# Float64 weights made float32 in two VectorE passes instead of three, with the words between them in a PSUM bank, and the low word's three bits by arithmetic on GpSimd

## The chip, the cores and the metric

The kernel runs on 1 core of one Trainium2 chip. The metric is the device time of one execution in microseconds, the median of several runs. A core has five engines with a queue of instructions each: TensorE (PE in the profile; PEld is its weight load), VectorE (DVE), ScalarE (ACT), GpSimd (POOL) and SyncE (SP), which here issues the DMAs. SBUF is the working memory; PSUM has eight banks of 512 float32 words per partition, into which TensorE writes.

## The reference

Windowed attention with 8 heads over 8 sequences of 576 positions, and then a feed-forward step with three up-projections of which the largest value is taken. The four weight matrices arrive as float64.

```python
scores = scale * np.matmul(q, k.transpose(0, 1, 3, 2))        # (8, 8, 576, 576), head_dim 64
# heads 0-3 see the last 32 keys, heads 4-7 every fourth of the last 128
scores = np.where(masks[None, :, :, :], scores, -1000000000.0)
attn = np.exp(scores - np.max(scores, axis=-1, keepdims=True))
attn = attn / (np.sum(attn, axis=-1, keepdims=True) + 1e-09)
x = np.matmul(attn, v)                                          # to (4608, 512)
h = np.maximum(np.maximum(x @ w1, x @ w2), x @ w3)              # w1, w2, w3: (512, 768)
out = h @ w_out                                                 # (768, 512)
```

## The kernel before

**Three kinds of work.** *Weights*: 24 chunks of the up-projections, 128 x 384 float64 numbers each, and 12 chunks of the down-projection, 128 x 256 each (`weight`, line 355). A chunk comes by DMA into a staging buffer `st`, is turned into float32, and is kept as two float32r parts, a high one (`wupH`, `wdn[:, 0]`) and a low one (`wupL`, `wdn[:, 1]`). *Attention*: 64 units of one half sequence (288 queries) and two heads (`attention`, line 432). The first 12 units are "lean": their scores come from plain float32 products. A later unit splits queries and keys into two parts `F` first. A unit's steps are scores into a bank `s` (TensorE), mask and row minimum (VectorE), exponential with row sum (ScalarE), reciprocal (VectorE), normalisation (GpSimd, or VectorE), transposition of the probabilities (TensorE for the first 8 units, into `pt`; then VectorE, line 672, into one of three buffers `PT`), products with the values into a bank `pv` (TensorE, line 684), and a copy `xH` (ScalarE or VectorE) and a remainder `xL` (VectorE) into a ring of four halves. *FFN*: 12 tiles of 384 tokens (`ffn`, line 715). A tile has 216 products `u` (line 729; 6 groups `f`, each needs 4 up chunks), whose maxima `tmp` VectorE takes, whose float32r parts `h` ScalarE and GpSimd make, and then 54 products `d` with the down weights (line 784) in three blocks of 128 tokens.

**How float64 becomes float32.** A float64 number is two 32-bit words, the low one first. Four steps work on the words: `rebias` (line 386; ScalarE, VectorE or GpSimd) reads the high word as if it were a float32 and multiplies it by 2^-112; `shift` (line 396, VectorE) drops the sign and moves the result up by three bits; `low` (line 399, VectorE) puts the low word's upper three bits under it; `sign` (line 407, VectorE) puts the sign back. All four write the same SBUF tile `c` (one of five buffers). Then `split` and a subtraction (line 423, GpSimd or VectorE) make the two float32r parts.

**What sets the order.** Nothing is written out by hand: `Plan.order` (line 147) gives each engine, by a rough clock with a cost per step, the step that is due first among those whose inputs and buffers are there. Steps that several engines can do carry a cost for each. The FFN's products are chained one after the other, and the due times of the other steps follow from theirs. So a change of a step's cost, engine or buffers moves the steps of all engines. Each engine then runs its queue in that order, with waits where the data or a buffer needs them.

**Banks.** `BANKS` (line 302) gives the eight PSUM banks to tags: scores `s` 2, `pt` 1, `pv` 2, FFN 3. A `pv` bank is free again when `xH` and `xL` of its unit have been read from it.

Of the kernel before, what the change touches and what calls it, by code (L numbers as in the profile page):

```python
# [10 lines left out]
U32 = mybir.dt.uint32  # L11
I64 = mybir.dt.int64
AF = mybir.ActivationFunctionType
ALU = mybir.AluOpType
# [13 lines left out]
# the first units have their scores from plain float32 products: fewer elementwise steps  # L28
# while the tensor engine has time
LEAN = 12  # L30
LEAN_B = -(-LEAN // (2 * NPAIR))
# up to this unit the tensor engine transposes the probabilities, then the vector engine
TURN = 8
# up to this half each head of a unit has its reciprocals apart
APART = 4
# buffers of the padded queries, and the unit up to which every other one's keys take a buffer of "F"
QPADS, KEYS_F = 4, 8
# weights are staged in the buffers of the down weights, every STAGE_H-th of those before STAGE_F in one of "h"
STAGE_F, STAGE_H = 13, 3
# the order of issue, in the plan's microseconds  # L40
SPILL = 2  # how much later its usual engine must be before a step goes to another
TO_PE = 0.26  # slack for inputs of the tensor engine
FFN_PACE = 1.267  # time that the FFN's products are given, over their own
UNIT_PACE, UNIT_SLACK, UNIT_LEAD = 1.146, 3.85, 3.484  # the same of attention, its margin, and a unit's to the next
# [3 lines left out]
def blocks_of(hf, dil):  # L48
    """Query blocks of one head's half: (first query column, queries, first key column, keys, mask offset)."""
# [22 lines left out]
class Buf:  # L72
    """A tile that a pool hands out when the first step that uses it is issued."""
# [16 lines left out]
class Step:  # L90
    """Instructions that one engine runs in a row; costs holds the engines that can, the usual one first."""
# [11 lines left out]
class Plan:  # L103
    """Puts the steps of all engines in an order of issue: each engine takes, of the steps whose
    inputs and buffers are there by a rough clock, the one that is due first. The waits that the
    data needs are Tile's."""
# [17 lines left out]
    def deadlines(self):  # L124
        """When steps are due: the FFN's products one after the other, the others as these need them."""
# [21 lines left out]
    def order(self):  # L147
# [11 lines left out]
        while len(order) < len(self.steps):  # L159
# [33 lines left out]
            else:  # L193
                cost = st.costs[e]
                if e == "pe":
                    # the tensor engine's clock is halved after a tick of its monitor that saw little work
# [39 lines left out]
def tile_dilated_window_attention__then__maxout_ffn(  # L236
# [41 lines left out]
    # key column kk is seen by query row qq when qq < kk <= qq + WIN  # L278
# [23 lines left out]
    BANKS = {"s": 2, "pt": 1, "pv": 2, "ffn": 3}  # L302
# [14 lines left out]
    # outside its band PT stays zero for good  # L317
# [31 lines left out]
    # ---------------------------------------------------------------- weights  # L349
# [5 lines left out]
    def weight(j, before):  # L355
        """Columns of float64 weights, turned into float32 and split into two float32r parts."""
# [15 lines left out]
        cb = buf("tmp", f"c{j}")  # L372
# [4 lines left out]
        def cf():  # L377
            return cb.t[:, :n]
# [3 lines left out]

        def like(ap):
            return ap.rearrange("p (g m) -> p g m", g=3) if up else ap

        def rebias(e):
            # the exponent's difference of 1023 - 127 is 112 units of the high word's own, which is 1/8 as fine
            h = st.t.rearrange("p (n t) -> p n t", t=2)[:, :, 1]
            if e == "act":
                nc.scalar.mul(cf(), h, REBIAS)  # L390
            elif e == "pool":
                nc.gpsimd.tensor_scalar(cf(), h, REBIAS, 1.0, ALU.mult, ALU.mult)
            else:
                nc.vector.tensor_scalar(cf(), h, REBIAS, None, ALU.mult)

        def shift(_):
            nc.vector.tensor_scalar(cw(), cw(), 0x0FFFFFFF, 3, ALU.bitwise_and, ALU.logical_shift_left)  # L397
# [497 lines left out]
```

## Time and profile before

| what | value |
|---|---|
| runs before | 775.7, 773.89, 774.74 us; median 774.74 |
| span of the profiled execution | 775.4 us |
| TensorE busy in the span | 730.6 us, 94% |
| VectorE, ScalarE, GpSimd busy | 482.5, 384.0, 406.4 us |
| mean granted TensorE clock | 0.978 |
| bytes moved | 72.75 MB, mean 94 GB/s |

The span goes from the first to the last instruction of one execution that was profiled on the chip. No separate time is listed for that execution; its span of 775.4 us lies between the slowest run and the median, 0.7 us above the median. Busy time is the time in which an engine works on an instruction, a wait inside an instruction included; a group's "mean ns" is the mean length of one instruction, and instructions that follow each other on one engine overlap a little in these records.

### The profile page before, as it was taken

What the parts mean: (1) busy time and instruction counts of PE and PEld (TensorE: products, weight loads), DVE (VectorE), ACT (ScalarE), POOL (GpSimd) and SP (SyncE); (2) the same over time, 40 slices, a digit from 0 to 9 for tenths busy, and PEclk for the clock granted to TensorE, in tenths of its full rate; (3) what the DMA queues carried; (4) which work ended last, traced back from release to release, by engine and by line L of the source; (5) the groups of instructions that cost most, each with busy time, mean ns of one, the idle gap of its engine ahead of it and who ended that gap; (6) DMA issues with size and microseconds to landing.
All of it is one profiled execution on the core that took longest, in us unless ns stands there. A gap on an engine that the chain in (4) does not pass through costs nothing.

```text
span 775.4 us, 14660 instructions
## 1 busy us (share of the span) xinstructions
PE 730.6 (94%) x4724; PEld 670.2 (86%) x4724; DVE 482.5 (62%) x1865; ACT 384.0 (50%) x1324; POOL 406.4 (52%) x560
## 2 busy tenths in 40 slices
PE   6787589999999999999999999999999999999998
PEld 5676578998998899799799799899699799899996
DVE  6899998888988879643884887511895611011110
ACT  7666466776766667552566477511465211111111
POOL 5877676787788588671288288611176011011110
PEclk9779898999999999999999999999999999999999
DMA  6974144344444433330433342410330200100001
GB/s 192 283 240 145 47 128 135 99 132 135 122 126 134 131 103 107 120 94 23 127 92 96 121 138 66 129 31 1 95 115 33 71 14 0 41 1 14 28 1 41
DMA packets 41516, 72.75 MB, mean 94 GB/s; under 512 B 4320, under 2 KB 15584, under 8 KB 41440
## 3 DMA queue, kind: packets, MB, share of 16 engines
q1 hardware_dynamic: 41440, 71.81, 30.3%
q8 instruction: 38, 0.62, 0.3%
q14 instruction: 38, 0.31, 0.1%
HBM read 62.36 MB, written 9.44 MB: 93 GB/s over the span
## 4 chain that ended last, share of the span: by engine, by line
PE 74%; DVE 19%; issue 3%; DMA 2%; POOL 1%; ACT 1%; SPq 0%; ACTq 0%; POOLq 0%; DVEq 0%
PE u L729 49%; PE d L784 15%; DVE PT L672 5%; PE s L533 5%; PE pv L684 3%; DVE c L408 3%; DVE c L400 3%; DVE W L560 2%; PE s L524 2%; DVE F L332 1%; DVE tmp L332 1%; DVE c L397 1%; DVE xL L332 1%; DMA st<-in_w_up_dram 1%; DVE W L546 1%
## 5 line engine op out<-in xcount | busy, mean ns | idle before, releaser
L332 POOL TENSOR_TENSOR F<-raw,F 64x288 fp32r<-64x288 f32 (+3 forms) x192 | 166.1, 867 | 81.2 <-ACT F L325 38.6
L332 DVE TENSOR_TENSOR tmp<-u,tmp 128x384 f32<-128x384 f32 x144 | 79.9, 555 | 203.0 <-PE u L729 200.4
L566 ACT ACTIVATE W<-W,mx 96x128 f32<-96x128 f32 (+3 forms) x448 | 166.5, 373 | 79.0 <-DVE mx L560 78.3
L729 PE MATMUL u<-xH,wupH 128*128 128x384 f32 x864 | 188.5, 339 | 7.2 <-DVE tmp L332 4.9
L729 PE MATMUL u<-xL,wupH 128*128 128x384 f32 x864 | 187.3, 338 | 0.0
L729 PE MATMUL u<-xH,wupL 128*128 128x384 f32 x864 | 186.4, 337 | 0.0
L332 POOL TENSOR_TENSOR h<-tmp,h 128x384 fp32r<-128x384 f32 x72 | 73.7, 1023 | 202.7 <-ACT h L325 201.7
L784 PE MATMUL d<-wdn,h 128*128 128x512 f32 x648 | 163.8, 401 | 0.0
L729 PEld LDWEIGHTS u<-xH,wupH 128*128 128x128 f32 x864 | 152.0, 189 | 11.2 <-DVE tmp L332 6.7
L729 PEld LDWEIGHTS u<-xL,wupH 128*128 128x128 f32 x864 | 152.1, 189 | 0.4
L729 PEld LDWEIGHTS u<-xH,wupL 128*128 128x128 f32 x864 | 151.5, 189 | 0.3
L672 DVE STREAM_TRANSPOSE PT<-W 32x192 f32<-32x192 f32 (+1 forms) x336 | 134.8, 401 | 13.0 <-PE pv L684 7.5
L784 PEld LDWEIGHTS d<-wdn,h 128*128 128x128 f32 x648 | 119.5, 191 | 24.6
L332 POOL TENSOR_TENSOR W<-W,sm 96x384 f32<-96x384 f32 (+2 forms) x127 | 103.5, 830 | 25.0 <-DVE sm L626 22.8
L325 ACT CAST h<-tmp 128x384 fp32r<-128x384 f32 x72 | 36.8, 511 | 131.2 <-DVE tmp L332 131.1
L566 ACT ACTIVATION_READ_ACCUMULATOR W<-W,mx 72x1 f32 (+1 forms) x448 | 84.1, 188 | 0.0
L325 ACT CAST F<-raw 128x576 fp32r<-128x576 f32 (+2 forms) x103 | 72.1, 704 | 18.2 <-DMA raw<-in_qk_d_dram 8.7
L560 DVE CUSTOM_DVE_ANT_0 W<-W,s 96x128 f32<-96x128 f32 (+2 forms) x364 | 76.6, 252 | 1.2
L546 DVE TENSOR_TENSOR W<-s,mask 72x208 f32<-72x208 f32 (+2 forms) x158 | 53.8, 361 | 28.2 <-PE s L533 26.1
L533 PE MATMUL s<-F 128*96 128x256 f32 (+3 forms) x364 | 59.9, 266 | 7.4 <-DVE mx L560 6.5
L533 PEld LDWEIGHTS s<-F 128*72 128x72 f32 (+1 forms) x364 | 47.0, 151 | 20.2 <-DVE mx L560 5.5
L684 PEld LDWEIGHTS pv<-PT,v 104*64 104x64 f32 (+1 forms) x896 | 36.6, 142 | 27.6 <-issue 15.3
(47 smaller groups left out, 502.6 us busy)
## 6 DMA issues: line engine op xcount, KB each, us to landing
raw<-in_qk_d_dram SPq DMA_DIRECT2D x28, 352.0 KB
st<-in_w_up_dram SPq DMA_DIRECT2D x24, 384.0 KB
out_dram<-o SPq DMA_DIRECT2D x36, 256.0 KB
raw<-in_qk_p_dram SPq DMA_DIRECT2D x28, 304.0 KB
raw<-in_qk_p_dram SPq DMA_DIRECT2D x24, 288.0 KB
raw<-in_qk_d_dram SPq DMA_DIRECT2D x24, 288.0 KB
v<-in_v_d_dram SPq DMA_DIRECT2D x32, 208.0 KB
v<-in_v_p_dram SPq DMA_DIRECT2D x32, 192.0 KB
```

Of the source, the lines that this page charges most:

```text
L325: nc.scalar.copy(dst, src)
L332: (nc.vector if eng == "dve" else nc.gpsimd).tensor_tensor(dst, a, b, op=op)
L400: nc.vector.scalar_tensor_tensor(cw(), words()[:, :, 0], 29, cw(), op0=ALU.logical_shift_right, op1=ALU.bitwise_or)
L408: nc.vector.scalar_tensor_tensor(cw(), words()[:, :, 1], 0x80000000, cw(), op0=ALU.bitwise_and, op1=ALU.bitwise_or)
L533: nc.tensor.matmul(bank.t[:nq, 256 * z : 256 * z + 2 * nk], f[:, q0 : q0 + nq], kv[:, :, k0 : k0 + nk], start=True, stop=True,)
L546: nc.vector.tensor_tensor(W3()[:nq, n0 : n0 + 2, mo : mo + nk], s3[:, :, :nk], m, op=ALU.add)
L560: nc.vector.tensor_tensor_reduce(a, x, y, -0.125, 3e38, ALU.add, ALU.min, mx.t[:nq, n : n + 1])
L566: nc.scalar.activation(a, a, AF.Exp, bias=mx.t[:nq, n : n + 1], scale=-1.0, accum_out=sm.t[:nq, n : n + 1])
L672: nc.vector.transpose(PT.t[c : c + 32, : 2 * nb, 32 * i : 32 * i + 32], W3(e)[32 * i : 32 * i + 32, :, c - e : c - e + 32],)
L684: nc.tensor.matmul(pv.t[64 * j : 64 * j + 64, q0 : q0 + nq], v.t[:wk, j, i, :], PT.t[:wk, nb * j + i, :nq], start=True, stop=True,)
L729: nc.tensor.matmul(bank.t[:, :n], wt[:, 3 * f + g, c, :], (xL if xz else xH)[:, c, r0 : r0 + n], start=(m == 0 and c == 0), stop=(m == 2 a ...
L784: nc.tensor.matmul(bank.t, hs[f].t[:, hz, s0 : s0 + 128], wdn[f].t[:, wz], start=(f == 0 and m == 0), stop=(f == NF - 1 and m == 2),)
```

## The change

`shift` and `low` go. `rebias` writes a tile `cp` in PSUM instead of `c`, and can run on ScalarE or VectorE only. A new step `low3` works on the staging buffer alone: it reads the byte that holds the low word's upper three bits, multiplies it by 1/32 and subtracts 31/64, and writes the result as an integer over the low word. GpSimd is its usual engine, VectorE the other. `joined` (VectorE) shifts the word in PSUM up by three bits, which drops the top bits, and puts the three bits under it, in place in PSUM. `sign` (VectorE) reads PSUM and the staging buffer and writes `c` in SBUF. `cp` has one bank, and `pv` has one where it had two. The costs that the plan is given are those that the steps of the same kind had. Comments were taken out as well, which moves line numbers by 1 to 12.

```diff
-    BANKS = {"s": 2, "pt": 1, "pv": 2, "ffn": 3}
+    BANKS = {"s": 2, "pt": 1, "pv": 1, "c": 1, "ffn": 3}
...
-        cb = buf("tmp", f"c{j}")
+        cb, cp = buf("tmp", f"c{j}"), buf("c", f"cp{j}")
...
             if e == "act":
-                nc.scalar.mul(cf(), h, REBIAS)
-            elif e == "pool":
-                nc.gpsimd.tensor_scalar(cf(), h, REBIAS, 1.0, ALU.mult, ALU.mult)
+                nc.scalar.mul(pf(), h, REBIAS)
             else:
-                nc.vector.tensor_scalar(cf(), h, REBIAS, None, ALU.mult)
-
-        def shift(_):
-            nc.vector.tensor_scalar(cw(), cw(), 0x0FFFFFFF, 3, ALU.bitwise_and, ALU.logical_shift_left)
-
-        def low(_):
+                nc.vector.tensor_scalar(pf(), h, REBIAS, None, ALU.mult)
+
+        def low3(e):
+            b = st.t.bitcast(U8).rearrange("p (n t) -> p n t", t=8)[:, :, 3]
+            (nc.gpsimd if e == "pool" else nc.vector).tensor_scalar(
+                words()[:, :, 0], b, 1 / 32, -31 / 64, ALU.mult, ALU.add
+            )
+
+        def joined(_):
             nc.vector.scalar_tensor_tensor(
-                cw(), words()[:, :, 0], 29, cw(), op0=ALU.logical_shift_right, op1=ALU.bitwise_or
+                pw(), pw(), 3, words()[:, :, 0], op0=ALU.logical_shift_left, op1=ALU.bitwise_or
             )
...
             nc.vector.scalar_tensor_tensor(
-                cw(), words()[:, :, 1], 0x80000000, cw(), op0=ALU.bitwise_and, op1=ALU.bitwise_or
+                cw(), words()[:, :, 1], 0x80000000, pw(), op0=ALU.bitwise_and, op1=ALU.bitwise_or
             )
...
-        first = s = plan.add({"act": act(n), "dve": dve(n), "pool": pool1(n)}, rebias, [s, before], [st, cb])
-        s = plan.add({"dve": dve2(n)}, shift, [s], [cb])
-        s = plan.add({"dve": dve(n)}, low, [s], [st, cb])
-        s = plan.add({"dve": dve(n)}, sign, [s], [st, cb])
+        first = plan.add({"act": act(n), "dve": dve(n)}, rebias, [s, before], [st, cp])
+        s = plan.add({"pool": pool1(n), "dve": dve(n)}, low3, [s, before], [st])
+        s = plan.add({"dve": dve(n)}, joined, [s, first], [st, cp])
+        s = plan.add({"dve": dve(n)}, sign, [s], [st, cp, cb])
```

The plan puts all 36 `low3` on GpSimd, 31 `rebias` on ScalarE and 5 on VectorE. The order moves on every engine. Three places:

**VectorE, around the first `tmp` of the first tile.** Before, a row with `tmp` as its output takes a maximum of the first tile, and nearly all else are weight passes:

```order
L400 SCALAR_TENSOR_TENSOR c_761<-st_293,c_761 128x384
L397 TENSOR_SCALAR c_776<-c_776 128x384
L408 SCALAR_TENSOR_TENSOR c_761<-st_293,c_761 128x384
L400 SCALAR_TENSOR_TENSOR c_776<-st_693,c_776 128x384
L397 TENSOR_SCALAR c_789<-c_789 128x384
L408 SCALAR_TENSOR_TENSOR c_776<-st_693,c_776 128x384
L332 TENSOR_TENSOR tmp_0_811<-u_0_1_793,tmp_0_811 128x384
```

Now, at the same first `tmp`:

```order
L412 SCALAR_TENSOR_TENSOR cp_843<-cp_843,st_658 128x384
L638 RECIPROCAL sm_729<-sm_729 96x3 x2
L420 SCALAR_TENSOR_TENSOR c_867<-st_658,cp_843 128x384
L638 RECIPROCAL sm_821<-sm_821 72x4
L330 CAST F_1_879<-raw_1_779 128x608
L333 TENSOR_TENSOR F_0_804<-raw_0_718,F_0_804 64x288
L333 TENSOR_TENSOR F_1_879<-raw_1_779,F_1_879 128x320
L333 TENSOR_TENSOR tmp_0_857<-u_0_1_846,tmp_0_857 128x384
```

The weight passes of a chunk now stand one after the other, and attention of later units (`F`, and below it masks and transposes) stands between the chunks.

**GpSimd, in the second half of the up chunks.** Before, the low parts of the weights (`wupL`) and little else:

```order
L332 TENSOR_TENSOR wupL<-c_837,wupH 128x3x128
L332 TENSOR_TENSOR wupL<-c_858,wupH 128x3x128
L332 TENSOR_TENSOR W_87<-W_87,sm_703 96x384
L332 TENSOR_TENSOR wupL<-c_882,wupH 128x3x128
L332 TENSOR_TENSOR W_87<-W_87,sm_703 96x384
L332 TENSOR_TENSOR h_1_963<-tmp_1_901,h_1_963 128x384
```

Now:

```order
L333 TENSOR_TENSOR wupL<-c_1092,wupH 128x3x128
L406 TENSOR_SCALAR st_881<-st_881 128x384
L333 TENSOR_TENSOR F_1_1134<-raw_1_1011,F_1_1134 128x320
L406 TENSOR_SCALAR st_973<-st_973 128x384
L333 TENSOR_TENSOR wupL<-c_1136,wupH 128x3x128
L333 TENSOR_TENSOR h_2_1167<-tmp_2_1080,h_2_1167 128x384
L633 TENSOR_TENSOR sm_1003<-sm_1003,eps_c 96x3
L333 TENSOR_TENSOR F_0_1027<-raw_0_901,F_0_1027 64x288
```

A `low3` (output `st`) per chunk came in, and the `F` remainders of later units.

**TensorE, at the end of the first tile's down products.** Rows `d_128` and `d_256` are the second and third block. Before:

```order
L784 MATMUL d_128_1428<-wdn_1366,h_5_1359 128x512 x3
L684 MATMUL pv_1501<-PT_93,v_1388 64x72 x8
L784 MATMUL d_256_1517<-wdn_1125,h_0_870 128x512 x3
L533 MATMUL s_2_1528<-F_1_1414 96x256 x2
L784 MATMUL d_256_1517<-wdn_1169,h_1_963 128x512 x3
```

Now:

```order
L796 MATMUL d_0_1525<-wdn_1735,h_5_1550 128x512 x3
L796 MATMUL d_128_1809<-wdn_1435,h_0_947 128x512 x3
L796 MATMUL d_128_1809<-wdn_1519,h_1_1059 128x512 x3
L545 MATMUL s_0_1839<-F_0_1801 96x256 x2
L696 MATMUL pv_1842<-PT_92,v_1713 64x96 x6
L796 MATMUL d_128_1809<-wdn_1588,h_2_1167 128x512 x3
L545 MATMUL s_1_1865<-F_0_1801 96x256
```

By the end of the first tile's `d` rows, TensorE has had 90 products `pv` and 12 products `s` of the later units before, and 118 and 52 now. In the later tiles two units' `pv` stand side by side before, and one `pv` behind every three rows of `d` now.

More of the change, by code (lines that the diff above doesn't have):

```diff
@@ L11 @@
 U32 = mybir.dt.uint32
+U8 = mybir.dt.uint8
 I64 = mybir.dt.int64
@@ L381, in cw, with pf, pw @@
             return cb.t.bitcast(U32)[:, :n]
+        def pf():
+            return cp.t[:, :n]
+        def pw():
+            return cp.t.bitcast(U32)[:, :n]
         def like(ap):
```

## The prediction

> **What bounds the kernel now.** I read the page's busy times and slices first, then cut the span into stages with the windows view.
>
> ```profile
> PE 730.6 (94%) x4724; PEld 670.2 (86%) x4724; DVE 482.5 (62%) x1865; ACT 384.0 (50%) x1324; POOL 406.4 (52%) x560
> ...
> PE   6787589999999999999999999999999999999998
> ...
> DVE  6899998888988879643884887511895611011110
> ...
> ```
>
> The first six slices (19.4 us each) hold nearly all of TensorE's missing time. In the windows view the columns behind the stage and its length are busy us of PE, PEld, DVE, ACT, POOL, then clock, DMA share and GB/s.
>
> ```profile
> 16.80:49.00 32.20, 23.24 (x233) 20.70 (x231) 28.66 (x129) 22.09 (x96) 23.34 (x37) 0.74 0.90 268
> 49.00:117.50 68.50, 51.95 (x276) 46.36 (x275) 67.99 (x150) 39.95 (x127) 49.45 (x59) 0.90 0.38 124
> 117.50:132.10 14.60, 14.60 (x94) 11.18 (x93) 12.87 (x51) 9.36 (x33) 10.40 (x16) 0.87 0.36 114
> 132.10:775.40 643.30, 629.37 (x4039) 581.88 (x4037) 362.37 (x1464) 299.37 (x1019) 314.21 (x425) 1.00 0.26 79
> ```
>
> The stages: 16.8 is the first weight step, 49.0 the first product `u`, 117.5 the end of the last down weight's low part, 132.1 the last `d` of the first tile. From 49.0 to 117.5 VectorE works 67.99 of 68.5 us, so it sets the pace. Before that DMA moves 268 GB/s at a share of 0.90. After 132.1 TensorE works 629.37 of 643.3 us. Rows of the chain of waits (start, length) price a whole tile and show the last product's end, 771.7:
>
> ```profile
> 659.66 12.38 PE d L784 x54
> 672.04 37.44 PE u L729 x216
> ...
> 759.30 12.39 PE d L784 x54
> ```
>
> The first tile takes 132.1 - 49.0 = 83.1 us where 37.44 + 12.38 = 49.8 would do. What a change to the weights can give lies in these 33 us, and in work of later units put into them.
>
> **What the change takes from VectorE.** The timeline shows why its weight passes are long; four rows of VectorE, then the two of GpSimd at that time.
>
> ```profile
> 56.73 1.36 DVE L408 SCALAR_TENSOR_TENSOR c<-st,c 128x384 uint32<-128x384 uint32 x1
> 58.01 0.55 DVE L400 SCALAR_TENSOR_TENSOR c<-st,c 128x384 uint32<-128x384 uint32 x1
> 58.48 0.35 DVE L397 TENSOR_SCALAR c<-c 128x384 uint32<-128x384 uint32 x1
> 58.75 1.40 DVE L408 SCALAR_TENSOR_TENSOR c<-st,c 128x384 uint32<-128x384 uint32 x1
> ...
> ```
> ```profile
> 56.55 1.13 POOL L332 TENSOR_TENSOR wupL<-c,wupH 128x384 fp32r<-128x384 f32 x1
> 58.71 1.02 POOL L332 TENSOR_TENSOR wupL<-c,wupH 128x384 fp32r<-128x384 f32 x1 [1.04 <-ACT wupH L325]
> ```
>
> A pass of 0.55 us takes 1.36 to 1.40 when a GpSimd subtraction started just ahead of it. These are the groups of 49.0 to 117.5 on VectorE (busy, mean ns):
>
> ```profile
> L408 DVE SCALAR_TENSOR_TENSOR c<-st,c 128x384 uint32<-128x384 uint32 x16 | 17.5, 1094 | 0.0
> L400 DVE SCALAR_TENSOR_TENSOR c<-st,c 128x384 uint32<-128x384 uint32 x15 | 12.0, 798 | 0.0
> L397 DVE TENSOR_SCALAR c<-c 128x384 uint32<-128x384 uint32 x15 | 10.3, 686 | 0.0
> L400 DVE SCALAR_TENSOR_TENSOR c<-st,c 128x256 uint32<-128x256 uint32 x12 | 7.8, 650 | 0.1
> L332 DVE TENSOR_TENSOR tmp<-u,tmp 128x384 f32<-128x384 f32 x12 | 6.5, 544 | 0.0
> L397 DVE TENSOR_SCALAR c<-c 128x256 uint32<-128x256 uint32 x12 | 6.5, 541 | 0.1
> L408 DVE SCALAR_TENSOR_TENSOR c<-st,c 128x256 uint32<-128x256 uint32 x12 | 5.5, 461 | 0.0
> ```
>
> The six weight groups make 59.6 us; all VectorE groups of the stage make 78.3, against 67.99 of time, since records overlap: a factor of 0.868. The `tmp` row has one input from PSUM and one from SBUF, and takes 0.544 us in the same stage, as if GpSimd were not there. `joined` and `sign` have that form. I take 0.55 for 384 elements. No row has this operation with PSUM as its output, nor 256 elements; for 256 I take 0.41, an estimate from 0.544 and the 0.448 of 288 elements below. The ends are 0.35 (the `shift` row without a neighbour) and 1.09 (the `sign` group). In the new order 15 up chunks and all 12 down chunks stand behind the first tile's last attention step, where 49.0 lies now: 30 x 0.55 + 24 x 0.41 = 26.3 us instead of 59.6, or 33.3 less.
>
> [...]
>
> **What the change puts there instead.** The freed time is not left empty. Up to the last `sign` the new order has on VectorE, beyond the old: 19 and 11 more transposes, 9 `F` remainders, 32 row minima of split units instead of 11 short ones, 16 masks, 6 more `xL`. The prices, from VectorE's groups after 117.5 and, for the last row, of the whole run:
>
> ```profile
> L672 DVE STREAM_TRANSPOSE PT<-W 32x256 f32<-32x256 f32 x168 | 73.0, 434 | 7.4 <-PE pv L684 4.6 <-POOL W L332 0.2
> L672 DVE STREAM_TRANSPOSE PT<-W 32x192 f32<-32x192 f32 x156 | 57.4, 368 | 5.4 <-PE pv L684 2.9 <-POOL W L332 0.6
> L560 DVE CUSTOM_DVE_ANT_0 W<-W,s 96x128 f32<-96x128 f32 x130 | 32.1, 278 | 0.7
> L332 DVE TENSOR_TENSOR xL<-pv,xH 128x288 fp32r<-128x288 f32 x55 | 24.3, 448 | 4.4 <-ACT xH L325 3.9
> ...
> L546 DVE TENSOR_TENSOR W<-s,mask 96x256 f32<-96x256 f32 x53 | 21.1, 413 | 10.2 <-PE s L533 9.7
> ...
> L332 DVE TENSOR_TENSOR F<-raw,F 64x288 fp32r<-64x288 f32 x14 | 13.4, 959 | 0.4
> ```
> ```profile
> L332 DVE TENSOR_TENSOR F<-raw,F 128x288 fp32r<-128x288 f32 x2 | 2.9, 1449 | 1.1 <-ACT F L325 1.1
> ```
>
> Transposes 19 x 0.434 + 11 x 0.368 = 12.3; remainders 6 x 0.959 + 3 x 1.449 = 10.1 (two SBUF inputs, so still held up); minima 32 x 0.278 and their reads, less the short ones, about 8; masks 16 x 0.39 = 6.2; `xL` 2.7; reciprocals, a cast and a normalisation about 3 (estimates). Sum 42. So 78.3 - 33.3 + 42 = 87.0, times 0.868 is 75.5 us for the stage where it is 68.5 now: 7 us longer.
>
> **GpSimd** gets all 36 `low3`. The rows nearest to it:
>
> ```profile
> L332 POOL TENSOR_TENSOR F<-raw,F 64x288 fp32r<-64x288 f32 x90 | 73.0, 813 | 48.3 <-issue 28.9 <-ACT F L325 10.8 <-POOL W L332 2.7
> ...
> L332 POOL TENSOR_TENSOR wupL<-c,wupH 128x384 fp32r<-128x384 f32 x24 | 27.1, 1133 | 12.7 <-ACT wupH L325 12.3
> ...
> L327 POOL TENSOR_SCALAR wupH<-c 128x384 fp32r<-128x384 f32 x4 | 2.0, 507 | 0.0
> ...
> L392 POOL TENSOR_SCALAR c<-st 128x384 f32<-128x384 f32 x3 | 1.7, 569 | 3.0 <-DMA st<-in_w_up_dram 3.0
> ```
>
> `L392` reads every other word of the same buffer, as `low3` reads every eighth byte; no row has a byte input or an integer output. I take 0.57 and, for 256, 0.46 (estimate); the ends are 0.51 (`L327`, the dense copy) and 1.13 (`wupL`, two inputs). In the stage that is 14 x 0.57 + 12 x 0.46 = 13.5 us. Ten more `F` remainders and 7 normalisations, two-input passes all, at 0.81 to 1.13 and taken as 0.87, add 15, small steps 1.5; a cast, two `wupL` and what the contention takes from GpSimd's own passes (`wupL` is 1.02 without it, 1.13 in the mean) go, about 7.5. So 49.45 + 22 = 71 of 75.5 us: nearly full as well. `low3` waits for its chunk's DMA and stands ahead of `wupL` and normalisations in one queue, and `joined` waits for it. For two nearly full engines that wait for each other I add 2 us (0 to 8): the stage ends at 49.0 + 77.5 = 126.5, 9 us later than now.
>
> Up to 49.0 VectorE loses about 6 us of passes by the same prices and GpSimd gains ten `low3` less three `rebias`, two `wupL` and two normalisations, about 7.5 us on 23.34 of 32.2; DMA is at 0.90 as before. I leave 49.0 where it is, with 3 us either way. ScalarE has room: 39.95 of 68.5 us. Its `rebias` stays but must wait for `sign` of the chunk ahead, as `cp` has one bank; exponentials queue behind it. The hidden cost is at most the chain of a chunk (0.55 `rebias`, 0.55, 0.55), 1.65 us x 27 = 45 us, which fits below 75.5.
>
> **TensorE at the first tile's end.** Of the 18 `d` rows, 12 stand behind the sixth, which needs the last down weight. Among them now stand 12 `s` and one unit's `pv`. From start to start:
>
> ```profile
> 124.18 0.39 PE L533 MATMUL s<-F 128*96 128x256 f32 x2
> 124.41 0.87 PE L784 MATMUL d<-wdn,h 128*128 128x512 f32 x3
> 125.11 0.40 PE L533 MATMUL s<-F 128*96 128x256 f32 x2
> ...
> 126.15 0.72 PE L684 MATMUL pv<-PT,v 104*64 104x72 f32 x16
> 126.80 0.95 PE L784 MATMUL d<-wdn,h 128*128 128x512 f32 x3
> ```
>
> Two `s` take 0.23, three `d` 0.70, a unit's `pv` 0.65. So 12 x 0.70 + 6 x 0.23 + 0.65 = 10.4 us: the tile ends at 136.9 instead of 132.1, 4.8 us later. But by then TensorE has done 40 `s` and 28 `pv` (four units) more: 20 x 0.23 + 4 x 0.65 = 7.2 us that the later tiles need not do.
>
> **After that.** TensorE idles 643.3 - 629.4 = 13.9 us, of which 3.7 lie behind its last product at 771.7. The rest lies mostly at bursts of `pv` and scores. With one `pv` bank, a unit's `xH` and `xL` (0.39 and 0.45 us) must be done before the next `pv`:
>
> ```profile
> L325 ACT CAST xH<-pv 128x288 fp32r<-128x288 f32 x63 | 24.3, 392 | 24.2 <-PE pv L684 13.8 <-PE u L729 9.4
> ```
>
> The new order puts three `d` rows (2.1 us) between, so I cost it at nothing; without that cover it is about 1 us for each of 64 units. Attention that is four units ahead gives TensorE fewer waits; I take 2 us off (0 to 5).
>
> **The sum.** Against the span: 775.4 + 4.8 - 7.2 - 2 = 771.0. The runs behind the median, 774.74, lie 0.7 us below the span, so 770.3.
>
> **The rivals.** *The stage does not grow.* If VectorE's new neighbours run undisturbed (the remainders at about 0.45 instead of 0.96 to 1.45), the first `u` comes 3 us earlier and nothing waits, the remainders take 5 us less of the stage, the 2 us of waits go, and the whole is 10 us better: 760, and 757 with the 5 us of later waits. For it: seven tenths of the work that GpSimd held up is gone. Against: GpSimd itself is at 71.
>
> *GpSimd becomes the bound* (slower). If `low3` costs 0.96 us, 26 of them add 10 us to 71, and `joined` and all queued behind wait; the stage takes 81 and, with 5 us of mutual waits, ends at 135: 8.5 us more than in the sum, 779, and 783 at 1.13. It decides from about 0.74 us, where GpSimd's time meets VectorE's 75.5. For it: its conversions and byte reads have no row; against: the undisturbed copy of the same buffer takes 0.51 to 0.57.
>
> *One `pv` bank stalls TensorE.* 0.2 us for each of the 47 units left is 9 us: 779. *Nothing is freed:* passes on PSUM are held up as before or slow at an output in PSUM; at 0.8 us instead of 0.55 and 0.6 instead of 0.41 all 54 cost 10 us of stage: 780. Against it stands the `tmp` row.
>
> **Chances.** Forecast 0.45 (767 to 775), no growth 0.22, GpSimd 0.18, `pv` bank 0.08, nothing freed 0.07. The range takes the first three to their ends: 757 to 784. A measurement can tell about 0.2%, 1.5 us, from no change, 773.2 to 776.3. Faster: 0.29 of the forecast and all of no growth, 0.51. Same: 0.12 and a part of the others, 0.17. Slower: 0.32.
>
> **What would show it.** Right: `joined` and `sign` near 0.55 us with little spread, VectorE and GpSimd both over 90% busy between the first `u` and the last `wdn`, that stage 74 to 80 us long, the first tile's end at 133 to 140, and a shorter remainder. Wrong: `low3` at 0.8 or more, passes on PSUM at 0.8, `pv` waiting for `xL` in the later tiles, or the first tile ending before 128.

## The result and the profile after

The changed kernel takes 788.24 us (median of 4 runs, 786.68 to 788.89) against 775.22 of the kernel before (the three runs shown above and a fourth of 779.74). The ratio on record is 1.015, interval 1.0126 to 1.0174; it is worked out from the single runs and is not the quotient of the two medians. It is slower, where 770.3 was forecast and 784 was the end of the range. The page of the changed kernel (busy times, then the busy tenths of TensorE and VectorE in 40 slices of 19.7 us):

```profile
PE 737.6 (94%) x4724; PEld 673.0 (86%) x4724; DVE 455.6 (58%) x1840; ACT 383.7 (49%) x1323; POOL 408.9 (52%) x586
...
PE   6679776999999989999999999999999999999998
...
DVE  6779998854886896212886887311887721011110
```

VectorE has 27 us less to do, and TensorE's thin slices reach to the seventh instead of the sixth. The same four stages in the windows view (length; busy PE, PEld, DVE, ACT, POOL; clock, DMA share, GB/s): to the first `u`, to the end of the last down weight's low part, to the last `d` of the first tile, and the rest.

```profile
16.80:53.09 36.29, 23.97 (x251) 20.51 (x249) 26.43 (x154) 26.58 (x118) 27.11 (x52) 0.82 0.91 278
53.09:130.50 77.41, 61.35 (x365) 53.68 (x364) 72.78 (x232) 54.92 (x181) 69.96 (x102) 0.83 0.47 143
130.50:146.00 15.50, 15.01 (x84) 12.03 (x85) 12.82 (x68) 11.11 (x40) 12.86 (x21) 0.84 0.51 152
146.00:787.10 641.10, 625.92 (x3943) 576.53 (x3941) 332.91 (x1315) 277.94 (x934) 290.12 (x387) 1.00 0.24 72
```

| stage (profiled us) | before | forecast | changed | off by |
|---|---|---|---|---|
| start to the first `u` | 49.0 | 49.0 | 53.1 | +4.1 |
| to the last low part | 68.5 | 77.5 | 77.4 | -0.1 |
| to the first tile's end | 14.6 | 10.4 | 15.5 | +5.1 |
| the other eleven tiles | 643.3 | 634.1 | 641.1 | +7.0 |
| span | 775.4 | 771.0 | 787.1 | +16.1 |

The stage on which the forecast spent most of its working came out to 0.1 us; three others did not. VectorE's costliest groups in that stage, then the two `low3` groups of GpSimd (busy, mean ns):

```profile
L684 DVE STREAM_TRANSPOSE PT<-W 32x256 f32<-32x256 f32 x24 | 10.4, 434 | 1.4 <-POOL W L333 0.8
L684 DVE STREAM_TRANSPOSE PT<-W 32x192 f32<-32x192 f32 x24 | 8.8, 368 | 0.5
L412 DVE SCALAR_TENSOR_TENSOR cp<-cp,st 128x384 uint32<-128x384 uint32 x15 | 8.2, 546 | 0.1
L420 DVE SCALAR_TENSOR_TENSOR c<-st,cp 128x384 uint32<-128x384 uint32 x15 | 8.1, 543 | 0.2
...
L412 DVE SCALAR_TENSOR_TENSOR cp<-cp,st 128x256 uint32<-128x256 uint32 x12 | 5.0, 420 | 0.1
L420 DVE SCALAR_TENSOR_TENSOR c<-st,cp 128x256 uint32<-128x256 uint32 x12 | 4.9, 406 | 0.1
```
```profile
L406 POOL TENSOR_SCALAR st<-st 128x384 uint32<-128x384 uint8 x14 | 7.9, 564 | 1.2
...
L406 POOL TENSOR_SCALAR st<-st 128x256 uint32<-128x256 uint8 x12 | 5.4, 450 | 1.0
```

Weight passes are 26.2 us in all (forecast 26.3), VectorE is busy for 72.8 of 77.4 us (75.5) and GpSimd for 70.0 (71). That the stage comes out to 0.1 us is partly luck: VectorE is busy for 2.7 us less than forecast, and idle for 4.6 us where 2 stood.

### The profile page after: what moved, and what is told of

Same layout as the page of the kernel before. It is cut to its first block, busy times and chain, and to the rows that moved or that the text cites. A ratio compares the mean times of both kernels' runs of the same rounds, so it can differ in the third digit from the quotient of the medians.

```text
span 787.1 us, 14709 instructions
## 1 busy us (share of the span) xinstructions
PE 737.6 (94%) x4724; PEld 673.0 (86%) x4724; DVE 455.6 (58%) x1840; ACT 383.7 (49%) x1323; POOL 408.9 (52%) x586
## 4 chain that ended last, share of the span: by engine, by line
PE 61%; DVE 14%; ACT 4%; POOL 3%; issue 2%; DMA 1%; ACTq 0%; POOLq 0%; DVEq 0%
PE u L741 45%; PE d L796 11%; DVE PT L684 9%; PE s L545 3%; POOL F L333 2%; ACT W L578 2%; PE pv L696 2%; DVE xL L333 1%; ACT F L326 1%; DVE W L572 1%; DVE W L558 1%; POOL W L333 1%; DVE F L333 1%; DMA raw<-in_qk_p_dram 1%; DVE tmp L333 0%
## 5 line engine op out<-in xcount | busy, mean ns | idle before, releaser
L333 POOL TENSOR_TENSOR F<-raw,F 64x288 fp32r<-64x288 f32 (+2 forms) x193 | 165.5, 858 | 71.0 <-issue 39.2
L578 ACT ACTIVATE W<-W,mx 96x128 f32<-96x128 f32 (+2 forms) x448 | 167.3, 375 | 71.9 <-DVE mx L572 71.2
L796 PE MATMUL d<-wdn,h 128*128 128x512 f32 x648 | 167.1, 404 | 1.3 <-DVE cp L412 0.7
L333 POOL TENSOR_TENSOR W<-W,sm 96x384 f32<-96x384 f32 (+2 forms) x121 | 96.7, 811 | 19.9 <-DVE sm L638 13.3
L572 DVE CUSTOM_DVE_ANT_0 W<-W,s 96x128 f32<-96x128 f32 (+3 forms) x364 | 75.8, 251 | 1.4
L696 PEld LDWEIGHTS pv<-PT,v 104*64 104x64 f32 (+1 forms) x896 | 38.2, 145 | 32.7 <-issue 13.9
```

The costliest lines, as they stand in the source:

```text
L333: (nc.vector if eng == "dve" else nc.gpsimd).tensor_tensor(dst, a, b, op=op)
L572: nc.vector.tensor_tensor_reduce(a, x, y, -0.125, 3e38, ALU.add, ALU.min, mx.t[:nq, n : n + 1])
L578: nc.scalar.activation(a, a, AF.Exp, bias=mx.t[:nq, n : n + 1], scale=-1.0, accum_out=sm.t[:nq, n : n + 1])
L696: nc.tensor.matmul(pv.t[64 * j : 64 * j + 64, q0 : q0 + nq], v.t[:wk, j, i, :], PT.t[:wk, nb * j + i, :nq], start=True, stop=True,)
L796: nc.tensor.matmul(bank.t, hs[f].t[:, hz, s0 : s0 + 128], wdn[f].t[:, wz], start=(f == 0 and m == 0), stop=(f == NF - 1 and m == 2),)
```

## The experiments

Each kernel computes the whole reference. Times are medians; the ratio is to the kernel before, run on the same chip, with its 95% interval. "First tile's end" is the start of the second tile's first `u`. "Beyond" is what the eleven later tiles take from there, up to the last product, beyond the products in them: 11 x 49.82 (one tile of the prediction's chain, 37.44 + 12.38), 0.115 us for each `s` and 0.081 for each `pv` instruction that the order puts there (the prediction's 0.23 for two `s`, 0.65 for eight `pv`; the trace has two records for each `pv` of the order). The other columns are read from each run's profiled execution.

| run | us | ratio | first `u` | first tile's end | beyond |
|---|---|---|---|---|---|
| before | 775.2 | 1 | 49.0 | 132.1 | 22.1 |
| changed kernel | 788.2 | 1.0150 (1.0126 to 1.0174) | 53.1 | 146.0 | 26.7 |
| e1 before, one `pv` bank | 786.8 | 1.0138 (1.0116 to 1.0160) | 54.3 | 141.0 | 24.5 |
| e2 two passes in SBUF | 780.6 | 1.0064 (1.0043 to 1.0085) | 53.5 | 137.2 | 22.1 |
| e3 word shares `pt`'s bank | 793.8 | 1.0238 (1.0202 to 1.0275) | 49.7 | 154.0 | 23.8 |
| e4 second `pv` bank later | 780.7 | 1.0058 (1.0037 to 1.0079) | 48.6 | 142.9 | 20.2 |
| e5 e4, attention held | 762.3 | 0.9818 (0.9794 to 0.9842) | 52.2 | 120.8 | 19.5 |
| e6 e4, held in part | 770.6 | 0.9926 (0.9901 to 0.9951) | 51.8 | 124.7 | 23.3 |
| e7 before, held | 777.5 | 1.0012 (0.9998 to 1.0026) | 50.2 | 130.0 | 23.6 |
| e8 e2, held | 779.3 | 1.0037 (1.0024 to 1.0051) | 51.3 | 126.8 | 26.4 |
| e9 changed, held | 765.3 | 0.9859 (0.9813 to 0.9905) | 49.9 | 117.9 | 23.1 |
| e10 e5, two word banks | 760.7 | 0.9793 (0.9755 to 0.9831) | 51.7 | 115.8 | 19.7 |
| e11 changed, `low3` on VectorE | 800.4 | 1.0297 (1.0259 to 1.0334) | 52.2 | 156.7 | 26.9 |
| e12 e10, a third of `low3` on VectorE | 764.5 | 0.9840 (0.9810 to 0.9871) | 50.2 | 116.5 | 23.9 |
| e13 changed, normalisations on GpSimd | 777.8 | 1.0014 (1.0002 to 1.0027) | 50.1 | 138.0 | 21.2 |
| e14 e9 with the rule of e13 | 761.6 | 0.9809 (0.9787 to 0.9831) | 51.7 | 119.7 | 16.9 |
| e15 e10, third score bank | 765.9 | 0.9862 (0.9844 to 0.9880) | 52.0 | 115.6 | 26.9 |
| e16 e14, two word banks | 756.7 | 0.9745 (0.9725 to 0.9766) | 51.0 | 115.3 | 17.8 |
| e17 e10 with the rule of e13 | 762.0 | 0.9812 (0.9795 to 0.9829) | 52.1 | 117.3 | 21.7 |
| e18 e17, `F` on GpSimd too | 758.1 | 0.9756 (0.9714 to 0.9798) | 51.3 | 116.2 | 16.4 |

### The bank or the crowding: e1 to e4

My theory after the result (A): the `pv` bank that was given away is the cost. The rival (B): the bank costs nothing, and GpSimd's new work and the attention pulled into the first tile do.

**e1.** The kernel before with one `pv` bank.

```diff
-    BANKS = {"s": 2, "pt": 1, "pv": 2, "ffn": 3}
+    BANKS = {"s": 2, "pt": 1, "pv": 1, "ffn": 3}
```

> The kernel before with one `pv` bank instead of two; its three weight passes stay. Theory A (the bank): the second `pv` bank given away is what costs. Then the later tiles, whose order of attention becomes that of the changed kernel, take about 5 us more in all, the first `u` comes up to 4 us later, and the time is 780 to 784. Theory B (crowding): the bank costs nothing, and the loss comes from GpSimd's `low3` and from attention that was put into the first tile while VectorE and GpSimd are both full. Then the time is within 2 us of the kernel before, 773 to 777.

786.8: almost the whole loss without any change to the weights. Ahead of the first `u` TensorE does wait for the bank, since `xL` of the unit ahead stands behind weight passes in VectorE's queue (TensorE's rows, then VectorE's):

```profile
47.38 1.78 PE L684 MATMUL pv<-PT,v 104*64 104x72 f32 x16
53.12 1.23 PE L684 MATMUL pv<-PT,v 104*64 104x72 f32 x16 [3.96 <-DVE xL L332]
```
```profile
48.59 1.36 DVE L400 SCALAR_TENSOR_TENSOR c<-st,c 128x384 uint32<-128x384 uint32 x1
...
51.55 1.15 DVE L397 TENSOR_SCALAR c<-c 128x384 uint32<-128x384 uint32 x1
52.62 0.44 DVE L332 TENSOR_TENSOR xL<-pv,xH 128x288 fp32r<-128x288 f32 x1
```

Theory A was off in the place: the first tile ends 8.9 us later, and the later tiles take only 2.4 us beyond their products more, not 5. The changed kernel loses its time in other places, so that the two totals lie so close says little.

**e2.** The changed kernel's arithmetic with the word in SBUF, in place, and two `pv` banks.

```diff
-        cb, cp = buf("tmp", f"c{j}"), buf("c", f"cp{j}")
+        cb = cp = buf("tmp", f"c{j}")
```

> The changed kernel's arithmetic (two VectorE passes, `low3` on GpSimd), but with the word in SBUF, in place, as the kernel before had it, and two `pv` banks again. Theory A: with both banks back and fewer passes it is faster than the kernel before, 768 to 773, though `joined` and `sign` with two SBUF inputs are held up again (mean 0.7 to 1.1 us). Theory B: GpSimd's ten `low3` before the first `u` delay it to about 53 all the same, and the time is 775 to 782.

780.6, theory B's range. One pass less gains nothing while the word lies in SBUF: behind the first `u`, `joined` takes 0.946 us on average and `sign` 0.685 (384 elements), and its tile is as long as before, 83.7 us.

**e3.** The changed kernel with two `pv` banks; the word takes turns with the early transposes.

```diff
-    BANKS = {"s": 2, "pt": 1, "pv": 1, "c": 1, "ffn": 3}
+    BANKS = {"s": 2, "pt": 1, "pv": 2, "ffn": 3}
...
-buf("c", f"cp{j}")
+buf("pt", f"cp{j}")
```

> The changed kernel with two `pv` banks: the word's bank is the one in which the first eight units' transposes land, taken in turn with them. Attention is put into the first tile as in the changed kernel (52 `s`, 62 `pv`). Theory A: first `u` near 49 to 51, later tiles 5 us shorter, 772 to 779. Theory B: the first tile is as long as in the changed kernel, 93 us, and the time stays at 784 to 789.

793.8, worse than either: the first `u` is early (49.7) as A had it, but the first tile takes 104.3 us. Until the last early transpose (44 us) the word has the bank only in turn, and 20 of the 24 up chunks are joined behind the first `u`, where the changed kernel has 15. So this run decides nothing between the two.

**e4.** From the ninth unit on, the bank of the early transposes serves as a second `pv` bank.

```diff
-        pv = buf("pv", f"pv{u}")
+        pv = buf("pt" if turned and u % 2 else "pv", f"pv{u}")
```

> The changed kernel, in which every second unit from the ninth on has its `pv` in the bank of the early transposes, which is free by then: one `pv` bank up to the first `u`, two behind it. Theory A: the first `u` stays near 53, the later tiles lose the 4 to 5 us that they took more, and the time is 780 to 785. Theory B: no change from the changed kernel, 787 to 789.

780.7, the lower edge of theory A's range. The rest behind the first tile is 634.5 us, as forecast (634.1); the first tile is not shorter:

```profile
16.80:48.56 31.76, 23.52 (x252) 20.39 (x250) 25.69 (x151) 25.96 (x117) 26.09 (x49) 0.84 0.97 295
48.56:127.40 78.84, 60.50 (x368) 51.96 (x365) 73.47 (x235) 54.98 (x183) 70.96 (x106) 0.86 0.49 149
127.40:142.90 15.50, 15.05 (x84) 12.03 (x85) 12.81 (x68) 11.20 (x41) 12.85 (x20) 0.84 0.53 151
142.90:777.40 634.50, 620.55 (x3943) 576.28 (x3941) 327.47 (x1314) 276.06 (x933) 289.06 (x388) 1.00 0.25 73
```

So neither theory holds alone. And one thing that neither had: up to the first `u`, e4 has the same instructions in the same order as the changed kernel, and reaches it at 48.6 instead of 53.1.

### What the crowding costs: e5 to e8, e11

Theory C: the attention that the order puts into the first tile is about 40 us of VectorE's time in the one stage that VectorE sets, and free later. D: the chain of the passes sets the first tile.

**e5** (with e4's edit besides) lets units from the 13th on load only behind the last chunk; in the code, behind its high part, the step after `sign`. **e6** spreads this, with `30 + 2 * (u - LEAN)` for the chunk. **e7** is the kernel before with the line of e5, **e8** e2 with it.

```diff
-            s = plan.add({"sp": 0.5}, load, bufs=[raw], nbytes=512 * w)
+            held = [w_of[min(NW - 1, 35 + 0 * (u - LEAN))][0]]
+            s = plan.add({"sp": 0.5}, load, held, [raw], nbytes=512 * w)
```

> As e4 (second `pv` bank from the ninth unit on), and besides every unit from the thirteenth on starts loading only when the last weight chunk has its sign: of attention the first tile keeps 8 `s` and 28 `pv` instead of 52 and 62. Theory C (crowding): the first tile is long because the order puts about 40 us of VectorE's attention into a stage in which VectorE and GpSimd set the pace, while the same work is free later. Then the first tile shrinks from 94 us to 65 to 78, the later tiles give back 6 to 9 us of TensorE's work, and the time is 758 to 772. Theory D (the passes themselves): the chain of `rebias`, `low3`, `joined`, `sign` and the split, with one bank for the word, sets the first tile. Then it stays above 85 us and the time is 778 or more.

> As e5, but the thirteenth unit may load after the 31st chunk and each next one two chunks later: the first tile keeps 16 `s` and 34 `pv`, about as much as in the kernel before (20 and 34). Theory C: between e4 and e5, nearer to e5, 760 to 775. Theory D: as e4, 778 to 783.

> The kernel before (three passes in SBUF, two `pv` banks) with the same hold as e5: 14 `s` and 28 `pv` in the first tile instead of 20 and 34. Theory C: only little is held back, so the first tile gets 2 to 5 us shorter, the later ones 1.2 us longer, 771 to 775; what e5 gains beyond that comes from the passes on PSUM. Theory D: no change, 774 to 777.

> Two passes with the word in SBUF (as e2) and the hold of e5. Theory C: its passes are held up by GpSimd (0.95 and 0.69 us on average in e2) and stay so, 14 us more of VectorE than on PSUM; the first tile lies 5 to 14 us above that of e5, the time at 768 to 779. If it is as fast as e5, the PSUM bank is worth nothing in itself and only the order counts.

e5 takes 762.3. The windows of e5 at the same stages:

```profile
52.16:109.20 57.04, 51.08 (x290) 44.10 (x288) 44.10 (x103) 35.67 (x104) 48.55 (x72) 0.92 0.38 119
109.20:120.80 11.60, 11.59 (x47) 9.42 (x48) 3.50 (x17) 6.15 (x19) 5.61 (x8) 0.83 0.40 121
120.80:762.50 641.70, 630.22 (x4056) 583.22 (x4054) 358.41 (x1481) 302.58 (x1034) 324.71 (x439) 1.00 0.27 81
```

VectorE's 73.5 us become 44.1, the first tile 68.6 us instead of 94.3, and the later tiles get 7.2 us longer: 25.7 us against 7.2. Theory C holds; e6 lies between, at the upper half of its range. The kernel before gains nothing from the hold (e7): its first tile gets 3.3 us shorter, as C had it, but the time (777.5, ratio 1.0012) does not fall; its later tiles take 1.5 us more beyond their products. e8 shows what PSUM does: with the word in SBUF the passes stay held up, and nothing is gained. VectorE's `joined` and `sign` over the whole run, first e8, then e5:

```profile
L412 DVE SCALAR_TENSOR_TENSOR c<-c,st 128x384 uint32<-128x384 uint32 x24 | 22.8, 967 | 1.4 <-ACT c L399 0.9 <-POOL st L406 0.6
L420 DVE SCALAR_TENSOR_TENSOR c<-st,c 128x384 uint32<-128x384 uint32 x24 | 22.3, 947 | 0.2
```
```profile
L412 DVE SCALAR_TENSOR_TENSOR cp<-cp,st 128x384 uint32<-128x384 uint32 x24 | 13.4, 559 | 3.9 <-ACT cp L399 2.2 <-POOL st L406 1.5
L420 DVE SCALAR_TENSOR_TENSOR c<-st,cp 128x384 uint32<-128x384 uint32 x24 | 13.1, 545 | 0.4
```

e8's time lies just above what was expected: its first tile is 6.9 us longer than e5's (75.5 to 68.6), and its later tiles too take 6.9 us more beyond their products. There the plan gives VectorE eight normalisations and thirteen remainders `F`, 21.0 us with both inputs in SBUF; e5 has one and nine, 7.9 us. The section on e13 to e18 shows what such passes cost.

**e11** puts all `low3` on VectorE in the changed kernel.

```diff
-        s = plan.add({"pool": pool1(n), "dve": dve(n)}, low3, [s, before], [st])
+        s = plan.add({"dve": dve(n)}, low3, [s, before], [st])
```

> The changed kernel with all 36 `low3` on VectorE instead of GpSimd; everything else, the one `pv` bank too, as in the changed kernel. If GpSimd were the bound of the first tile (the forecast's rival), taking 18.6 us from it would shorten that tile by several us: 780 to 785. If VectorE, crowded with attention, is the bound, its 36 further passes at about 0.5 us make the first tile longer by 8 to 14 us: 794 to 802.

800.4: taking work from GpSimd gains nothing and giving it to VectorE costs, as it should if VectorE sets the first tile, which becomes 104.5 us long. The tile grows by 11.6 us, as expected, though the 36 passes cost 26.5 us, 0.74 each instead of 0.5.

### Bank and crowding apart, and the word's own bank: e9, e10, e12

**e9** is the changed kernel with e5's hold and its one `pv` bank; **e10** is e5 with a second bank for the word; **e12** is e10 with `{"dve": dve(n)}` for every third `low3`.

```diff
-        cb, cp = buf("tmp", f"c{j}"), buf("c", f"cp{j}")
+        cb, cp = buf("tmp", f"c{j}"), buf("pt" if j >= 12 and j % 2 else "c", f"cp{j}")
```

> The changed kernel with one `pv` bank throughout, and the hold of e5 alone. If the two causes add up, it stands to e5 (762.3) as the changed kernel to e4 (788.2 to 780.7): 769 to 771. If the one bank costs only where attention is crowded, it equals e5, 761 to 764. If the bank is the greater cause also without crowding, 773 or more.

> As e5, with a second bank for the word: every odd chunk from the 13th on uses the bank of the early transposes. In e5 ScalarE's `rebias` waits 13.3 us for `sign` of the chunk ahead and VectorE's `joined` 7.4 us for `rebias`. If that chain sets the first tile once the crowding is gone, the first tile is 4 to 8 us shorter, 754 to 759. If GpSimd sets it (54.1 of 57 us busy behind the first `u` in e5), no more than 2 us come, 760 to 763.

> As e10, with every third `low3` on VectorE. If GpSimd sets the first tile when attention is held and the word has two banks, taking 6 us from it brings 2 to 5 us: 751 to 758. If not, it equals e10 within 2 us or is slower.

e9, at 765.3, is 3.0 us above e5, with intervals that overlap: between its first two cases, undecided by the time. Its trace has 3.6 us more beyond the products. e10's first tile is 4.5 us shorter than e5's (64.1 to 68.6), at the lower end of the first case, but its time (760.7, intervals overlapping with e5's) lies in the second case's range: the trace shows the chain, the time does not resolve it. Later traces bear the chain out: the first tile takes 63.6 to 65.2 us in the five runs with two word banks, the full hold and `low3` on GpSimd (e10, e15 to e18), and 68.0 to 68.6 in the three with one (e5, e9, e14). The waits of e5 behind its first `u` that the second bank thins out:

```profile
ACT cp L399 <- DVE c L420: 13.3, 17, 1.7
DVE cp L412 <- ACT cp L399: 7.4, 12, 1.0
```

e12 is no faster than e10: GpSimd does not set the first tile there.

### Why one bank costs in the later tiles: e13 to e18

In the later tiles no `pv` row of the changed kernel waits for the bank. TensorE's longest wait there, and VectorE and GpSimd ahead of it:

```profile
473.79 0.86 PE L741 MATMUL u<-xH,wupH 128*128 128x384 f32 x4
476.60 0.43 PE L545 MATMUL s<-F 128*72 128x208 f32 x2 [1.95 <-DVE mx L572]
476.82 1.52 PE L741 MATMUL u<-xL,wupH 128*128 128x384 f32 x4
```
```profile
469.88 3.08 DVE L333 TENSOR_TENSOR W<-W,sm 96x384 f32<-96x384 f32 x1
473.06 2.28 DVE L684 STREAM_TRANSPOSE PT<-W 32x192 f32<-32x192 f32 x6
```
```profile
469.70 0.82 POOL L333 TENSOR_TENSOR W<-W,sm 96x384 f32<-96x384 f32 x1
470.49 1.08 POOL L333 TENSOR_TENSOR F<-raw,F 128x416 fp32r<-128x416 f32 x1
471.53 1.02 POOL L333 TENSOR_TENSOR h<-tmp,h 128x384 fp32r<-128x384 f32 x1
```

A normalisation that the plan gave to VectorE (two SBUF inputs) takes 3.08 us beside three GpSimd passes in a row; the transposes and score reads behind it are late, TensorE waits 1.95 us, and its next four products take 1.52 us instead of 0.86 (the granted clock is 0.50 from 476.8 to 480.2). In the changed kernel's later tiles the plan gives VectorE six such normalisations (the expectation of e13 counts the one above twice); in e4's it gives one. The six:

```profile
L333 DVE TENSOR_TENSOR W<-W,sm 96x384 f32<-96x384 f32 x6 | 9.9, 1645 | 0.1
```

Theory E: these are the cost. F: the one bank as such is. **e13** is the changed kernel with

```diff
-            done = plan.add({"pool": 0.06 + 0.00195 * n, "dve": dve(n)}, norm, [r, cleared], [W, sm])
+            done = plan.add({"pool": 0.06 + 0.00195 * n} if turned else {"pool": 0.06 + 0.00195 * n, "dve": dve(n)}, norm, [r, cleared], [W, sm])
```

and **e14** is e9 with the same. **e15** is e10 with `buf("c" if u >= 16 and g % 3 == 2 else "s", f"s{u}_{g}")` for the scores' bank.

> The changed kernel, one `pv` bank, in which normalisations from the ninth unit on may run on GpSimd alone. In the changed kernel's later tiles the plan gives seven of them to VectorE, six at 1.65 us on average and one at 3.08 us just ahead of TensorE's longest wait (1.95 us). Theory E (what the single bank costs later is these): the later tiles lose 4 to 6.5 us, as with the second bank, 781 to 785. Theory F (one bank as such, the order of `pv` and scores): no more than 1.5 us, 786 to 789. The first `u` stands behind the same instructions as in the changed kernel (53.1) and e4 (48.6): where it comes now says how far it scatters.

> As e9 (one `pv` bank, hold), with the same rule for normalisations as e13. Theory E: the later tiles shorten by 3 to 4 us, to those of e5, 760 to 763. Theory F: no change, 764 to 767.

> As e10, and from the 17th unit on every third group of scores lands in the bank that the word no longer needs. TensorE's waits for scores in the later tiles are 3.3 to 4.5 us. If they come from the two score banks, 2 to 4 us go: 756 to 759. If VectorE is late by itself, nothing changes: 759 to 763.

e13 takes 777.8, within 0.3% of the kernel before, and better than theory E had it. The fourth tile, which the seventh repeats, in the changed kernel and in e13:

```profile
270.60:331.90 61.30, 57.54 (x347) 52.98 (x346) 39.86 (x172) 35.01 (x129) 42.66 (x58) 1.00 0.33 100
```
```profile
266.70:323.90 57.20, 56.84 (x348) 53.11 (x347) 33.66 (x167) 35.34 (x128) 44.88 (x62) 1.00 0.35 107
```

With the same 346 products in each (a window counts one or two more at its edges), VectorE has 6.2 us less and the tile is 4.1 us shorter; the seventh is 4.4 us shorter. In both tiles the counts differ only in three normalisations and one remainder, which went from VectorE to GpSimd. The third, fifth, sixth and eighth to twelfth tile have the same instructions in both runs and take the same time to 0.05 us, so this is not scatter. The second tile is 4.0 us longer in e13: 1.2 us are products that the first tile no longer does, and it has four remainders on VectorE instead of two. Of the 12.4 us between the two spans, 4.4 lie in the later tiles, 3.0 ahead of the first `u` (the same instructions, so scatter) and 5.0 in the first tile, whose order also has six `s` and six `pv` less. e14 (761.6) agrees: 6.2 us less beyond the products than e9, more than the 3 to 4 expected, though by time it is 3.7 us and the intervals overlap. e15 is slower than e10, against both cases: its order again has six normalisations on VectorE behind the first tile, and fourteen remainders.

**e16** is e14 with e10's second word bank; **e17** differs in the second `pv` bank alone.

> One `pv` bank, the hold of e5, normalisations on GpSimd alone as in e13, and two banks for the word as in e10. If the three are independent, its first tile is e10's (64.1 us) and its later tiles are e14's (635.4 to the last product): 754 to 758. If the one `pv` bank still costs something of its own, it lies 2 us or more above e17.

> As e16, with the second `pv` bank of e4. If the bank as such is worth something beside the place of the normalisations, it is 2 us or more faster than e16; if not, equal to it, 754 to 759.

e16, with one `pv` bank, is the fastest of all: 756.7, as expected, 2.5% below the kernel before. e17 is 5.3 us slower, against what was expected of it. Its one long wait (2.21 us) stands behind the same kind of pass, this time a remainder, on VectorE:

```profile
453.88 3.33 DVE L333 TENSOR_TENSOR F<-raw,F 64x288 fp32r<-64x288 f32 x1
```
```profile
461.58 0.59 PE L546 MATMUL s<-F 128*72 128x208 f32 x2 [2.21 <-DVE mx L573]
```

**e18** keeps these off VectorE as well, from the 21st unit on.

```diff
-plan.add({"pool": pool(HALF), "dve": dve(HALF)}, qlow
+plan.add({"pool": pool(HALF), "dve": dve(HALF)} if u < 20 else {"pool": pool(HALF)}, qlow
```

and the same for `klow`.

> As e17 (two `pv` banks), and from the 21st unit on the remainders `F` may run on GpSimd alone too. In e17 a remainder on VectorE takes 3.33 us, and TensorE's longest wait (2.21 us, for scores) and a slower clock come behind it; e16 has no such wait. If such passes are what makes e17 5 us slower than e16, it comes to 756 to 759; if two `pv` banks are worse in themselves or something else is the reason, it stays at 760 to 763.

758.1, within the first case, and level with e16 (0.9756 and 0.9745). The seventh tile, 61.9 us in e17, takes 57.2 in e18. In the later tiles two-input passes on VectorE are what sets these runs apart, and whether there are one or two `pv` banks is not. Over all twenty traces the time that VectorE spends behind the first tile on normalisations and remainders goes with "beyond" (correlation 0.92), from 0 us and 16.4 in e18 to 22.0 and 26.9 in e15. It does not give the size of each: the changed kernel has 15.6 us of them, e4 10.4, but the kernel before 17.1 at 22.1 beyond.

## Why the prediction was wrong, step by step

- **The passes** were right. `joined` and `sign` cost 0.55 and 0.41 to 0.42 us; 26.2 us where 26.3 stood. "Nothing is freed" falls: with one of the two inputs in PSUM 384 elements took 0.545 to 0.559 us in e5, near the `tmp` row (0.544) from which the forecast had its price, and with both in SBUF 0.947 to 0.967 in e8.
- **GpSimd** was right: `low3` at 0.564 and 0.450, 70.0 of 77.4 us. That it becomes the bound falls with e11 and, with attention held, e12.
- **The stage** was right: 77.4 for 77.5, with somewhat less work and more idle time than forecast. The prediction saw that VectorE's gain is given to attention and still counted that as nearly neutral. e5 shows the true price: the same attention left for later costs 7.2 us there and frees 25.7 here.
- **"I leave 49.0 where it is, with 3 us either way"**: 53.1. The changed kernel, e4 and e13 run the same instructions up to that point and reach it at 53.1, 48.6 and 50.1. Nine further runs (e5, e6, e9, e10, e14 to e18) give TensorE, VectorE, ScalarE and GpSimd the same work up to there, with two loads fewer, and reach it at 49.9 to 52.2; the median of the twelve is 51.7. The order of the kernel before takes 49.0 and, in e7, 50.2. So about 2 of the 4.1 us are likely the change's and the rest scatter; with two traces on one side this is not settled. The first row that differs clearly between the changed kernel and e4 is a `low3` that waits for its chunk's DMA (GpSimd's rows, changed kernel first):

```profile
19.77 0.53 POOL L406 TENSOR_SCALAR st<-st 128x384 uint32<-128x384 uint8 x1 [1.66 <-DMA st<-in_w_up_dram]
```
```profile
18.89 0.53 POOL L406 TENSOR_SCALAR st<-st 128x384 uint32<-128x384 uint8 x1 [0.73 <-DMA st<-in_w_up_dram]
```

- **"So 12 x 0.70 + 6 x 0.23 + 0.65 = 10.4 us: the tile ends at 136.9"** failed, by 5.1. Behind the last weight stood 13.3 `d` rows, 16 `s` and two units' `pv`: 9.3 + 1.8 + 1.3 = 12.4 us at the prediction's prices. And the granted clock was lower than in the rows that gave those: in the windows from 126 to 138 TensorE works for 1.91 of the first four us, and the granted clock is 0.50 into the third. It is 0.50 from 115.0 to 135.5 here, and in the kernel before from 114.4 to 121.2; the rows that gave the prices stand behind that, from 124 to 127, at 1.00.

```profile
126.00:130.00 4.00, 1.91 (x4) 0.89 (x4) 3.06 (x9) 1.68 (x5) 3.84 (x6) 0.50 0.20 64
130.00:134.00 4.00, 3.47 (x24) 3.07 (x25) 3.10 (x17) 2.52 (x10) 2.84 (x6) 0.50 0.40 128
134.00:138.00 4.00, 3.61 (x23) 2.55 (x22) 3.23 (x15) 2.71 (x10) 3.69 (x6) 0.82 0.43 136
```

  Half the clock for 3.5 us and 0.82 for 4 lose 2.5 us (worked out from these rows), idle time about 0.5.
- **"7.2 us that the later tiles need not do" and "2 us off"**: 9.2 forecast, 2.2 measured. The work was indeed done ahead (40 `s` and 28 `pv` by the order), and e4 has 8.8. What failed is "I cost it at nothing", the single `pv` bank's term. Its rival named 9 us, near the 7.0 that were missing, but by waits of `pv` for `xL`, which these tiles do not show: with one bank the plan moves normalisations to VectorE, six in the changed kernel, five in e1 and six in e9, where e4, the kernel before and e5 have one (e13 and e14 show what that costs). The plan does so with two banks too in some runs (six in e7, eight in e8), so the bank is one way to that order and not the only one. In the first stage of e1 the wait that the rival named is there, 3.96 us.

The slip common to the last two: I priced where work goes by its duration, and left out both the granted clock of 0.50 at which TensorE was running and the steps queued behind one long pass. Why the plan gives VectorE normalisations when it has one `pv` bank was not tried out. Nor was the rule of e13 tried on the kernel before, whose later tiles have 17.1 us of two-input passes on VectorE: of what e16 gains, some 4 us (22.1 to 17.8 beyond the products) might be had without the change.

## What to carry to other kernels

Time freed on the engine that sets a stage is worth something only if the planner does not fill it with work that would be free elsewhere: here the same cheaper passes cost 1.5% with the planner's order and gain 2.5% with the early attention held back, normalisations kept on GpSimd and a second bank for the word. A resource given up (a bank) can show its price through the planner, as steps on another engine, with no wait for that resource in the tiles that pay it: look for what else moved. Where GpSimd is busy, let VectorE's passes take one of their two inputs from PSUM (0.545 to 0.559 us in e5 instead of 0.947 to 0.967 in e8), or keep passes with two SBUF inputs off it where other engines wait behind them (one took 3.08 us in the changed kernel, and TensorE waited 1.95 us). One SBUF input alone was no safeguard here, as `low3` on VectorE shows below (2.735 us at the most in e11).

## What the runs showed of the hardware

- In the changed kernel, between the first `u` and the last low part, a VectorE pass that reads and writes the same PSUM bank in place, with one SBUF operand, took 0.546 us for 384 elements and 0.420 for 256 in the mean, beside 0.543 and 0.406 from PSUM to SBUF.
- A VectorE pass with two SBUF inputs took 3.08 us in the changed kernel beside three GpSimd passes in a row (0.82, 1.08 and 1.02 us) and ended 0.4 us behind the third; one such normalisation in the first tile took 0.543, beside a GpSimd pass (`h`) that took 1.55.
- `low3` on VectorE (e11), one SBUF input, took 0.280 us at the least, 0.451 in the median and 2.735 at the most, both sizes together: 0.280 for 256 elements and 0.354 to 0.369 for 384 while GpSimd was idle, and 2.735 beside three GpSimd passes in a row (0.83, 1.00 and 1.08 us).
- The same instructions up to the first `u`, where DMA is at 0.91 to 0.97 in the changed kernel and e4, took 48.6, 50.1 and 53.1 us in three traces. Behind the first tile, tiles with the same instructions in the changed kernel and e13 agree to 0.05 us.
